# Attention and a gated product on one core: batch 1's score matmuls of two pairs in three visits, one head pair's masks moved to VectorE

## The chip, the cores and the metric

One of the cores of a Trainium2 chip runs the whole program. The time is device time in microseconds (us), the median of three runs. One more execution is profiled, and everything that is said here of single instructions is from that one.

## The reference

Blockwise causal attention over 8 batches, 8 heads, 576 positions and 64 columns a head; its result, laid out as 4608 rows of 512, goes through a gated product with 2048 columns in the middle.

```python
# q, k, v: (8, 8, 576, 64); block = 64
scores = scale * np.matmul(q, k.transpose(0, 1, 3, 2))
mask = (pos[:, None] // block) >= (pos[None, :] // block)
scores = np.where(mask, scores, -1000000000.0)
attn = np.exp(scores - scores.max(-1, keepdims=True))
attn = attn / (attn.sum(-1, keepdims=True) + 1e-09)
x = np.matmul(attn, v).transpose(0, 2, 1, 3).reshape(4608, 512)
# w_in: (512, 2048); w_out: (2048, 512); beta: (2048,)
h = x @ w_in
out = (h * (1.0 / (1.0 + np.exp(-beta * h)))) @ w_out
```

## The kernel before

**The plan.** The program is not written in the order in which it runs. Python code adds operations to a planner `P`: each with its engine, an estimated duration, what it depends on, the tiles that it holds and a priority. The planner picks, engine by engine, the operation that can start and has the lowest priority number, gives tiles their places, and so fixes the order of each engine's instructions. On the chip an engine runs that order from front to back and waits where a semaphore is not yet there: an instruction that waits holds up all behind it.

**Attention.** A pair is two heads, numbered u = 4b + c for batch b and c from 0 to 3, so that batch 0 has pairs 0 to 3 and batch 1 has pairs 4 to 7; the fourth pair is pair 3. The Q and K of batches 0 and 1 come in by one DMA for each of Q and K of a pair, are turned into bfloat16 (L731), transposed by TensorE (L742, four matmuls against an identity) and copied out of PSUM (L752). From batch 2 on (`b >= QB`) they come for two pairs at once and a DMA transposes them (L783, on SyncE's queue).

The scores are computed transposed, keys on the partitions. A pair's scores have four parts by key block: part 0 (512 query columns), part 1 (64 and 448), part 2 (320 and 192) and part 3 (64). The two heads of a pair lie on the two halves of the array's rows, and the code hands the matmuls of both halves out in turn (L837, and L457, which repeats a matmul with weights that are there). What the planner moves as one operation is called a visit here. Where `b` is not in `JOIN`, a pair has two visits, of parts (0, 1) and of parts (2, 3). Where it is, two pairs have three: (0, 1) of the first, (2, 3) of both (the joined visit), (0, 1) of the second. Each visit's parts 0 to 2 need a pair of PSUM banks each, the small part 3 a single one. ScalarE takes the exponential (L857; L872 for part 3), and masks are memsets that put zeros over the blocks above the diagonal (L865, L867): on VectorE, but for the first two parts of batch 0's pairs, which are on GpSimd.

The value product of a pair (L1051, 30 matmuls) holds a pair of banks: banks 0, 2, 4 or 6 on where `b` is in `JOIN`, else 0 or 2 (`pv.at`). VectorE takes the reciprocal of the sums (L1063) and normalises (L1070) into `xq`; TensorE transposes that (L1099, five matmuls) and VectorE copies it into `xT` (L1109). From batch 3 on a DMA transposes `xq` (L1087, SyncE's queue). The last 64 rows of batch 0 are done apart (L975 to L1038, the late rows).

**The gated product** goes in nine chunks of 512 rows. A chunk has sixteen groups of four matmuls of `xT` and a quarter of `w_in` (L1297), each group with one single bank of PSUM (four to seven, in turn as they come free); ScalarE takes a tanh of it (L1307), VectorE combines the two into `gT` (L1311), and then the bank is free. The output of chunk 0 is the product with `w_out` in groups of four matmuls (L1333); other chunks use a scheme of fewer products (L1214, with sums by VectorE, L1178). Groups of chunk 0 fill TensorE between the scores of batch 1; the fifth is the first that needs the second quarter of `w_in`. The quarters of `w_in` (L524) and of `w_out` (L529) are issued on GpSimd's queue, between its casts and masks. A few matmuls on zeros (L548) fill places in which the planner expects TensorE to stand.

Of the kernel before, what the change touches and what calls it, by code (L numbers as in the profile page):

```python
# [11 lines left out]
NPAIR = 4  # L12
# [347 lines left out]
def bass_blockwise_causal_attn__then__act_swish_beta_kernel(  # L360
# [10 lines left out]
    with es:  # L371
# [9 lines left out]
        JOIN = (2,3,4,5,6,7)  # L381
# [271 lines left out]
        copied, more0 = [], []  # L653
        early6, rows = [], []
        QKI, QKX = 550, 2700
        for u in range(NU):
# [10 lines left out]
            if b < QB:  # L667
# [50 lines left out]
                turned = []  # L718
                for w, (nm, src) in enumerate((("Q", q), ("K", k))):
                    ts, pt = P.tile("ST"), P.tile("P1")  # L720
                    early6.append(ts)

                    def fl(g, e, ts=ts, src=src, b=b, c=c):
                        return [g.dma_start(STm[ts.slot].rearrange("p h j d -> p h (j d)"),  # L724
                                            src[b, 2 * c:2 * c + 2, 0:512].rearrange("h (p j) d -> p h (j d)", j=4))]

                    o = ld[nm, u] = P.op("SP", 540, fl, tiles=[ts], xfer=(760, 950)[b], prio=u, dma=["d_S", 0, 1])
                    o.pkt = 48.0

                    def fn(g, e, ts=ts, tn=tn, p=p, w=w):  # L730
                        return g.tensor_copy(QKn[tn.slot][:, p, w, 0:512].rearrange("p (j h d) -> p j h d", j=4, h=2),  # L731
                                             STm[ts.slot].rearrange("p h j d -> p j h d"))

                    onp = u not in (0, 3) or w == 1
                    o = P.op("POOL" if onp else "DVE", 620 if onp else 430, fn, deps=[o], tiles=[ts, tn],
                             prio=-40 + 3 * u if onp else -1)
                    if u == 4:
                        kcast4 = o

                    def ft(g, e, tn=tn, pt=pt, p=p, w=w):  # L740
                        for i in range(4):
                            z = g.transpose(PSb[:, pt.slot, 128 * i:128 * i + 128],  # L742
                                            QKn[tn.slot][:, p, w, 128 * i:128 * i + 128], identB[:])
                        return z

                    o = P.op("PE", 4 * 56, ft, deps=[o, c4], tiles=[tn, pt, tt_], lat=4 * 56 + 170, mode="full",
                             prio=pr(u))

                    def fc(g, e, pt=pt, td=tt_, p=p, w=w):
                        x, y = (QKT[td.slot][:, p, w, 0:512].rearrange("c (p j) -> c p j", j=4),  # L750
                                PSb[:, pt.slot, 0:512].rearrange("c (j p) -> c p j", j=4))
                        return g.activation(x, y, ACT.Copy) if e == "ACT" else g.tensor_copy(x, y)  # L752

                    o.rest = 400.0 if b else 0.0
                    held4 = held4 + [o] if u == 4 else [] if u < 4 else held4
                    held_t = held_t + [o] if u == 5 else [] if u < 5 else held_t

                    turned.append(P.op(("DVE", "ACT") if u in (4, 5) else "DVE", dve_t(512) + 30, fc, deps=[o], tiles=[pt, tt_], prio=-5 if b < 1 else .5))
# [28 lines left out]
            tqk, cps = tt_, turned  # L787
# [3 lines left out]
            if b not in JOIN or p == 0:  # L791
# [6 lines left out]
                for grp in visits:  # L798
# [46 lines left out]
                    o = P.op("PE", n, fq, deps=cps + more, tiles=list({id(x): x for x in pst}.values()) + [tqk] + [tes[uu] for uu in sorted({uu for uu, _ in grp})] * (b > 0),  # L845
# [5 lines left out]
            for g0 in range(4 if b else 3):  # L851
                o, ps = qk[g0]
                if g0 < 3:
# [14 lines left out]
                    zs.append(P.op("DVE" if b or g0 == 2 else "POOL", 160 if g0 != two else 220, fz, deps=[x], tiles=[te], prio=-20 if b or g0 == 2 else -37))  # L868
# [558 lines left out]
```

## Time and profile before

| what | value |
|---|---|
| median of 3 runs | 328.6 us (328.39 to 328.95) |
| the profiled execution: its time | 329.3 us |
| its span | 327.5 us |
| TensorE busy | 316.4 us, 97% |
| VectorE, ScalarE, GpSimd busy | 219.9, 211.8, 84.5 us |
| chain that ended last | 83% TensorE, 5% DMA, 4% VectorE, 4% ScalarE |

The span goes from the first to the last record of the profiled execution; its time is taken around it, on the device too. The chain follows the work that ended last back to what released it, so it tells on which engine the span was spent, and not what a gain there is worth. In rows of the timeline, neighbouring instructions of one line stand together (x4), and a row's length is from the start of the first to the end of the last; since matmuls overlap, a row ends a little after the next has started.

### The profile page before, as it was taken

Reading aid. Unit: us, or ns where it says so; the run is one execution under the profiler, and the core shown is the slowest. Engines: PE = TensorE matmul, PEld = TensorE weight load, DVE = VectorE, ACT = ScalarE, POOL = GpSimd, SP = SyncE. Lnnn points to the kernel's source line nnn. Section 1 sums busy time; section 2 is a strip of 40 time slices with the busy share of each in tenths; the row PEclk is TensorE's granted clock in tenths of the full one; section 3 lists DMA queues with packets and bytes.
Section 4 is the critical chain, followed back from the end, with each engine's and each line's share of the span. In section 5 each row is a group of like instructions: output and inputs, shape, how many; then the busy total and the mean of one; then the engine's idle time right before and its main releaser. Section 6 shows DMA issues by size and latency. Waiting matters only on the chain.

```text
span 327.5 us, 7435 instructions
## 1 busy us (share of the span) xinstructions
PE 316.4 (97%) x3101; PEld 200.3 (61%) x3012; DVE 219.9 (67%) x455; ACT 211.8 (65%) x312; POOL 84.5 (26%) x137
## 2 busy tenths in 40 slices
PE   7698999999999999999999999999999999999996
PEld 2454446445786457854776467666666766666695
DVE  5657857578763789368843996659576866666742
ACT  2769891388557886499657866885978454544521
POOL 4768090073073046103520541150000000000000
PEclk9999999999999999999999999999999999999999
DMA  7999999999999999997999999999030310111023
GB/s 224 225 302 233 215 211 199 169 292 189 226 252 221 222 193 218 186 240 152 196 190 241 231 197 195 199 169 152 0 74 2 104 34 32 62 36 35 6 92 128
DMA packets 156706, 53.58 MB, mean 164 GB/s; under 512 B 139120, under 2 KB 156160, under 8 KB 156672
## 3 DMA queue, kind: packets, MB, share of 16 engines
q1 hardware_dynamic: 144112, 40.46, 65.8%
q10 hardware_dynamic: 8336, 8.46, 8.2%
q0 software_dynamic: 4224, 4.19, 7.8%
q8 instruction: 24, 0.39, 0.5%
q14 instruction: 10, 0.08, 0.1%
HBM read 36.71 MB, written 9.44 MB: 141 GB/s over the span
## 4 chain that ended last, share of the span: by engine, by line
PE 83%; DMA 5%; DVE 4%; ACT 4%; issue 2%; SPq 1%; POOL 1%; POOLq 0%
PE PS L1297 34%; PE PS L1214 29%; PE PS L1051 8%; PE PS L837 6%; PE PS L1333 4%; DMA w_in<-in_moe_w_in_dram 3%; ACT E L857 2%; DMA ST<-in_q_dram 2%; DVE gT L1311 1%; ACT th L1307 1%; DVE QKT L752 1%; SPq L724 1%; DMA xT<-xq 1%; PE PS L1099 1%; PE PS L912 0%
## 5 line engine op out<-in xcount | busy, mean ns | idle before, releaser
L1297 PE MATMUL PS<-xT,w_in 128*128 128x512 bf16 x576 | 137.7, 379 | 3.1 <-DMA w_in<-in_moe_w_in_dram 1.2
L1307 ACT ACTIVATE th<-PS,beta 128x512 f32<-128x512 f32 x144 | 97.0, 701 | 54.9 <-PE PS L1297 53.9
L1311 DVE SCALAR_TENSOR_TENSOR gT<-th,PS 128x512 f16<-128x512 f32 x144 | 95.2, 681 | 35.8 <-ACT th L1307 35.4
L857 ACT ACTIVATE E<-PS 128x1024 bf16<-128x1024 f32 (+1 forms) x90 | 87.5, 1014 | 22.4 <-PE PS L837 21.5
L1297 PEld LDWEIGHTS PS<-xT,w_in 128*128 128x128 bf16 x576 | 53.1, 98 | 58.5 <-issue 2.2
L1214 PE MATMUL PS<-w_out,gT 128*128 128x256 f16 x512 | 63.0, 273 | 0.1
L1214 PEld LDWEIGHTS PS<-w_out,gT 128*128 128x128 f16 x512 | 49.0, 98 | 12.1 <-issue 0.8
L776 POOL CAST QKn<-ST 128x640 bf16<-128x640 f32 x48 | 37.0, 771 | 24.9 <-DMA ST<-in_k_dram 13.9
L624 POOL CAST Vn<-Vs 128x640 bf16<-128x640 f32 x24 | 19.6, 815 | 91.7 <-DMA Vs<-in_v_dram 90.6
L1236 ACT ACTIVATE ost<-PS 128x512 f32<-128x512 f32 x32 | 19.3, 604 | 28.5 <-PE PS L1214 28.5
L1214 PE MATMUL PS<-OV 128*128 128x256 f16 (+1 forms) x264 | 31.8, 270 | 0.0
L1051 PEld LDWEIGHTS PS<-Vn,E 128*128 128x128 bf16 x810 | 27.5, 97 | 3.9 <-issue 0.4
L837 PE MATMUL PS<-QKT 64*128 64x448 bf16 (+7 forms) x292 | 28.6, 295 | 0.5 <-ACT E L857 0.5
L1051 PE MATMUL PS<-Vn,E 128*128 128x65 bf16 x810 | 28.4, 193 | 0.0
L1214 PEld LDWEIGHTS PS<-OV 128*128 128x128 f16 x264 | 24.5, 98 | 6.1 <-issue 0.6
L1178 DVE TENSOR_TENSOR OV<-gT 128x1024 f16<-128x1024 f16 x32 | 23.9, 753 | 0.6
L837 PEld LDWEIGHTS PS<-QKT 64*128 64x128 bf16 (+1 forms) x292 | 13.3, 94 | 17.7 <-issue 3.6
L1070 DVE TENSOR_TENSOR xq<-PS,inv 128x640 bf16<-128x640 f32 x28 | 23.0, 820 | 0.5
L1239 DVE SCALAR_TENSOR_TENSOR ost<-PS,ost 128x512 f32<-128x512 f32 x22 | 15.2, 689 | 9.5 <-PE PS L1214 6.9
L865 DVE MEMSET E<- 64x64 uint32 x57 | 6.3, 112 | 17.9 <-ACT E L857 16.0
L1214 PE MATMUL PS<-OV,gT 128*128 128x256 f16 (+1 forms) x136 | 16.0, 266 | 0.0
L1333 PE MATMUL PS<-w_out,gT 128*128 128x512 f16 x64 | 15.3, 379 | 0.0
(106 smaller groups left out, 189.9 us busy)
## 6 DMA issues: line engine op xcount, KB each, us to landing
out_dram<-ost ACTq DMA_DIRECT2D x32, 256.0 KB, 3.9
ST<-in_q_dram SPq DMA_DIRECT2D x12, 576.0 KB, 6.2
ST<-in_k_dram SPq DMA_DIRECT2D x12, 576.0 KB, 7.2
Vs<-in_v_dram SPq DMA_DIRECT2D x24, 256.0 KB, 4.6
ST<-in_q_dram SPq DMA_DIRECT2D x8, 256.0 KB, 5.9
ST<-in_k_dram SPq DMA_DIRECT2D x8, 256.0 KB, 6.1
w_in<-in_moe_w_in_dram POOLq DMA_DIRECT2D x4, 512.0 KB, 8.4
w_out<-in_moe_w_out_dram POOLq DMA_DIRECT2D x4, 512.0 KB, 8.9
```

The costliest lines, as they stand in the source:

```text
L624: return g.tensor_copy(Vn[t.slot][:, 0:n, g0:g1, 0:64], Vs[ts.slot][:, 0:n, g0:g1, :])
L776: return g.tensor_copy(QKn[tn.slot][:].rearrange("p a w n -> p (a w n)")[:, 640 * (2 * a + w):][:, 0:640] .rearrange("p (t h d) -> p t h d ...
L837: z = g.matmul(o, QKT[tqk.slot][r, uu % 2, 1, k0:k0 + m], x)
L857: return g.activation(E3[es_(te)][:, g0, :, 0:n], PS[:, ps.slot:ps.slot + 2, 0:n], ACT.Exp, scale=0.125)
L1051: z = g.matmul(o, eblk(te, t, i, h), Vn[Tv.slot][:, t, 2 * c + h, 0:65], start=(t == 0), stop=(t == i))
L1070: return g.tensor_tensor(xq[xq_(tx)][:].rearrange("p i (h d) -> p h i d", h=2), both(pv, 0, 64), x, ALU.mult)
L1178: return P.op("DVE", dve_t(SZ * HC / 2), mk(lambda g: g.tensor_tensor(fo(), fx(), fy(), op)), deps=deps, tiles=tiles, prio=prio)
L1214: x = g.matmul(PS[:, pw.slot, HM * w + c0:HM * w + c1], fa()[:, j, 128 * w:128 * w + 128], fb()[:, j, c0:c1], start=first and (pair or w = ...
L1297: z = g.matmul(PS[:, ph.slot, :], w_in[:, c, 128 * j:128 * j + 128], xT[:, c, row % RX:row % RX + RC], start=(c == 0), stop=(c == 3))
L1307: return g.activation(th[tt.slot][:], PS[:, ph.slot, :], ACT.Tanh, scale=beta[:, j:j + 1])
L1311: return g.scalar_tensor_tensor(out=gT[tg.slot][:, j, :], in0=th[tt.slot][:], scalar=1.0, in1=PS[:, ph.slot, :], op0=ALU.add, op1=ALU.mult)
L1333: z = g.matmul(PS[:, po.slot, 0:d1 - d0], gT[tg.slot][:, j, 128 * w:128 * w + 128], w_out[:, j, d0:d1], start=(j == 0), stop=(j == NJ - 1))
```

## The change

Batch 1 is put into `JOIN`. Its scores, until now four pairs of two visits, become twice three. For that the code of batches 0 and 1 makes the loads, casts, transposes and copies of pairs u and u + 1 when it comes to the first of them (`vu`), and the copies are kept by pair (`turns`), so that a visit depends on the copies of its pairs alone. The value products of batch 1 may now take any of four pairs of banks. Apart from it, the masks of pair 3 that GpSimd wrote go to VectorE, with VectorE's priority.

```diff
-        JOIN = (2,3,4,5,6,7)
+        JOIN = (1, 2, 3, 4, 5, 6, 7)
...
-        copied, more0 = [], []
+        copied, more0, turns = [], [], {}
...
-                turned = []
-                for w, (nm, src) in enumerate((("Q", q), ("K", k))):
+                for vu, w, nm, src in [(vu, w, *z) for vu in ((u,) if b not in JOIN else (u, u + 1) if p == 0 else ())
+                                      for w, z in enumerate((("Q", q), ("K", k)))]:
+                    cv, pu_ = vu % NPAIR, vu % 2
...
-                    o = ld[nm, u] = P.op("SP", 540, fl, tiles=[ts], xfer=(760, 950)[b], prio=u, dma=["d_S", 0, 1])
+                    o = ld[nm, vu] = P.op("SP", 540, fl, tiles=[ts], xfer=(760, 950)[b], prio=vu, dma=["d_S", 0, 1])
...
-                    turned.append(P.op(("DVE", "ACT") if u in (4, 5) else "DVE", dve_t(512) + 30, fc, deps=[o], tiles=[pt, tt_], prio=-5 if b < 1 else .5))
+                    turns.setdefault(vu, []).append(P.op(("DVE", "ACT") if vu in (4, 5) else "DVE", dve_t(512) + 30, fc, deps=[o], tiles=[pt, tt_], prio=-5 if b < 1 else .5))
...
-            tqk, cps = tt_, turned
+            tqk = tt_
...
-                    o = P.op("PE", n, fq, deps=cps + more, tiles=list({id(x): x for x in pst}.values()) + [tqk] + [tes[uu] for uu in sorted({uu for uu, _ in grp})] * (b > 0),
+                    o = P.op("PE", n, fq, deps=(turned if b >= QB else [o for uu in sorted({uu for uu, _ in grp}) for o in turns[uu]]) + more, tiles=list({id(x): x for x in pst}.values()) + [tqk] + [tes[uu] for uu in sorted({uu for uu, _ in grp})] * (b > 0),
...
-                    zs.append(P.op("DVE" if b or g0 == 2 else "POOL", 160 if g0 != two else 220, fz, deps=[x], tiles=[te], prio=-20 if b or g0 == 2 else -37))
+                    zs.append(P.op("DVE" if b or g0 == 2 or u == 3 else "POOL", 160 if g0 != two else 220, fz, deps=[x], tiles=[te], prio=-20 if b or g0 == 2 or u == 3 else -37))
```

From the joined loop on, a line of the changed kernel has the number of before plus one (L837 is L838, and so on to the end).

**TensorE, around the second quarter of w_in.** Before, the order has here the fourth L1297 group, pair 4's visit (2, 3), a transpose of pair 5, the fifth group (the first that needs the second quarter), the late rows' value product and the next visit (2, 3), pair 5's.

```order
L1297 MATMUL PS<-xT,w_in 128x512 x4
L837 MATMUL PS<-QKT 128x320 x2
L837 MATMUL PS<-QKT 128x192 x2
L837 MATMUL PS<-QKT 64x64 x2
L742 MATMUL PS<-identB,QKn 128x128 x4
L1297 MATMUL PS<-xT,w_in 128x512 x4
L1007 MATMUL PS<-Vn,gT 128x65 x40
L837 MATMUL PS<-QKT 128x320 x2
L837 MATMUL PS<-QKT 128x192 x2
L837 MATMUL PS<-QKT 64x64 x2
L742 MATMUL PS<-identB,QKn 128x128 x12
```

Now, from the second half of pair 4's visit (0, 1) on, there is the fourth group, a filler, pair 5's last transpose ahead of its scores, the fifth group, the joined visit and two transposes, and then the sixth group.

```order
L1298 MATMUL PS<-xT,w_in 128x512 x4
L548 MATMUL PS<-zero 128x256
L743 MATMUL PS<-identB,QKn 128x128 x4
L1298 MATMUL PS<-xT,w_in 128x512 x4
L838 MATMUL PS<-QKT 128x320 x2
L838 MATMUL PS<-QKT 128x192 x2
L838 MATMUL PS<-QKT 128x320 x2
L838 MATMUL PS<-QKT 128x192 x2
L838 MATMUL PS<-QKT 64x64 x4
L743 MATMUL PS<-identB,QKn 128x128 x8
L1298 MATMUL PS<-xT,w_in 128x512 x4
```

The visit (2, 3) of pair 4 has moved from ahead of the fifth group to behind it, where it is one with pair 5's.

**TensorE, at the end of batch 1.** Before, the last groups of L1297, the four value products and the transposes L1099 alternate, and L1333 starts behind the last value product.

```order
L1297 MATMUL PS<-xT,w_in 128x512 x8
L1051 MATMUL PS<-Vn,E 128x65 x60
L1297 MATMUL PS<-xT,w_in 128x512 x8
L1099 MATMUL PS<-identB,xq 128x128 x5
L1051 MATMUL PS<-Vn,E 128x65 x30
L1099 MATMUL PS<-identB,xq 128x128 x5
L1051 MATMUL PS<-Vn,gT 128x65 x30
L1333 MATMUL PS<-w_out,gT 128x512 x8
L1099 MATMUL PS<-identB,xq 128x128 x5
```

Now three value products stand in a row, the transposes of pairs 4, 5 and 6 follow with one group of L1333 between them, and pair 7's visit (0, 1) comes after those.

```order
L1298 MATMUL PS<-xT,w_in 128x512 x8
L1052 MATMUL PS<-Vn,E 128x65 x90
L1100 MATMUL PS<-identB,xq 128x128 x5
L1334 MATMUL PS<-w_out,gT 128x512 x4
L1100 MATMUL PS<-identB,xq 128x128 x10
L838 MATMUL PS<-OV 128x512 x2
L457 MATMUL PS<-OV 128x64 x2
L838 MATMUL PS<-OV 128x448 x2
L1334 MATMUL PS<-w_out,gT 128x512 x16
```

The two groups of L1297 that stood between the value products now stand ahead of them, and a visit and the fourth value product have moved behind the transposes.

**VectorE, in the same place.** Before, the combines L1311 stand between the reciprocals, normalisations and copies of single pairs.

```order
L1311 SCALAR_TENSOR_TENSOR gT<-th,PS 128x512
L1063 RECIPROCAL inv<-PS 128x10
L1070 TENSOR_TENSOR xq<-PS,inv 128x2x5x64
L1311 SCALAR_TENSOR_TENSOR gT<-th,PS 128x512
L1109 COPY xT<-PS 128x512
L1109 COPY xT<-PS 128x64
L1311 SCALAR_TENSOR_TENSOR gT<-th,PS 128x512
L1063 RECIPROCAL inv<-PS 128x10
L1109 COPY xT<-PS 128x512
L1109 COPY xT<-PS 128x64
L1070 TENSOR_TENSOR xq<-PS,inv 128x2x5x64
```

Now the last combine comes first, and the reciprocals and normalisations of pairs 5 and 6 stand two by two.

```order
L1312 SCALAR_TENSOR_TENSOR gT<-th,PS 128x512
L1064 RECIPROCAL inv<-PS 128x10 x2
L1110 COPY xT<-PS 128x512
L1110 COPY xT<-PS 128x64
L1071 TENSOR_TENSOR xq<-PS,inv 128x2x5x64 x2
L1110 COPY xT<-PS 128x512
L1110 COPY xT<-PS 128x64
L1110 COPY xT<-PS 128x512
L1110 COPY xT<-PS 128x64
```

Both normalisations stand behind the copies of pair 4, and the copies of pairs 5 and 6 behind both.

## Rows read from the trace of the kernel before

**Rows 1.** The page, busy us of each engine (share of the span) and instructions.

```profile
PE 316.4 (97%) x3101; PEld 200.3 (61%) x3012; DVE 219.9 (67%) x455; ACT 211.8 (65%) x312; POOL 84.5 (26%) x137
```

**Rows 2.** TensorE's waits from 45 us on: us in total, times, longest us.

```profile
PE PS L1297 <- DVE xT L1109: 0.6, 1, 0.6
...
PE PS L837 <- ACT E L857: 0.2, 1, 0.2
```

**Rows 3.** Timeline of TensorE near 31 us: start us, us, instruction, [idle <-releaser].

```profile
27.97 1.03 PE L1297 MATMUL PS<-xT,w_in 128*128 128x512 bf16 x4
28.96 0.54 PE L837 MATMUL PS<-QKT 64*128 64x320 bf16 x6
29.43 0.40 PE L742 MATMUL PS<-identB,QKn 128*128 128x128 bf16 x4
31.00 1.04 PE L1297 MATMUL PS<-xT,w_in 128*128 128x512 bf16 x4 [1.18 <-DMA w_in<-in_moe_w_in_dram]
...
34.84 0.39 PE L837 MATMUL PS<-QKT 64*128 64x512 bf16 x2 [0.34 <-ACT E L857]
```

**Rows 4.** Timeline of GpSimd (POOL) ahead of 22 us.

```profile
19.01 0.20 POOL L865 MEMSET gT<- 64x128 bf16 x1
...
19.76 0.62 POOL L731 CAST QKn<-ST 128x512 bf16<-128x512 f32 x1
21.47 0.74 POOL L524 DMA_DIRECT2D w_in<-in_moe_w_in_dram  x1 [1.09 <-DMA ST<-in_k_dram]
```

**Rows 5.** Timeline of TensorE at the end of batch 1.

```profile
43.38 1.04 PE L1297 MATMUL PS<-xT,w_in 128*128 128x512 bf16 x4 [0.40 <-DVE gT L1311]
...
44.89 1.90 PE L1297 MATMUL PS<-xT,w_in 128*128 128x512 bf16 x8
46.62 1.97 PE L1051 MATMUL PS<-Vn,E 128*128 128x65 bf16 x60
...
51.34 0.44 PE L1099 MATMUL PS<-identB,xq 128*128 128x128 bf16 x5
...
52.53 1.89 PE L1333 MATMUL PS<-w_out,gT 128*128 128x512 f16 x8
```

**Rows 6.** Timeline of ScalarE (ACT) in batch 1's scores.

```profile
40.03 1.99 ACT L857 ACTIVATE E<-PS 128x1024 bf16<-128x1024 f32 x2
41.84 1.34 ACT L1307 ACTIVATE th<-PS,beta 128x512 f32<-128x512 f32 x2
...
43.99 1.37 ACT L1307 ACTIVATE th<-PS,beta 128x512 f32<-128x512 f32 x2
```

**Rows 7.** Timeline of TensorE, a joined visit of a later batch.

```profile
117.02 0.67 PE L837 MATMUL PS<-QKT 64*128 64x64 bf16 x12
```

**Rows 8.** Timeline of VectorE (DVE), the combine of the group at 31.00.

```profile
32.80 0.69 DVE L1311 SCALAR_TENSOR_TENSOR gT<-th,PS 128x512 f16<-128x512 f32 x1 [1.24 <-ACT th L1307]
```

**Rows 9.** Timeline of VectorE at the end of batch 1.

```profile
49.74 0.21 DVE L1063 RECIPROCAL inv<-PS 128x10 f32<-128x10 f32 x1
49.99 0.82 DVE L1070 TENSOR_TENSOR xq<-PS,inv 128x640 bf16<-128x640 f32 x1
50.73 0.68 DVE L1311 SCALAR_TENSOR_TENSOR gT<-th,PS 128x512 f16<-128x512 f32 x1
51.33 0.52 DVE L1109 COPY xT<-PS 128x512 bf16<-128x512 bf16 x2
```

**Rows 10.** Timeline of GpSimd, the first issue for w_out.

```profile
40.57 0.74 POOL L529 DMA_DIRECT2D w_out<-in_moe_w_out_dram  x1 [7.74 <-DMA OV<-in_v_dram]
```

**Rows 11.** Timelines of SyncE's queue (SPq) and TensorE, two late waits.

```profile
104.32 1.04 PE L1297 MATMUL PS<-xT,w_in 128*128 128x512 bf16 x4 [0.62 <-DVE xT L1109]
...
162.38 4.81 SPq L783 DMA_TRANSPOSE QKT<-QKn  x1
167.23 2.55 SPq L1087 DMA_TRANSPOSE xT<-xq  x2
...
170.92 1.90 PE L1297 MATMUL PS<-xT,w_in 128*128 128x512 bf16 x8 [0.61 <-DMA xT<-xq]
```

More of the change, by code (lines that the diff above doesn't have):

```diff
@@ L717, in bass_blockwise_causal_attn__then__act_swish_beta_kernel, with fl, fn, ft @@
                     tail = tailc[c // 2]
-                turned = []
-                for w, (nm, src) in enumerate((("Q", q), ("K", k))):
+                for vu, w, nm, src in [(vu, w, *z) for vu in ((u,) if b not in JOIN else (u, u + 1) if p == 0 else ())
+                                      for w, z in enumerate((("Q", q), ("K", k)))]:
+                    cv, pu_ = vu % NPAIR, vu % 2
                     ts, pt = P.tile("ST"), P.tile("P1")
                     early6.append(ts)
-                    def fl(g, e, ts=ts, src=src, b=b, c=c):
+                    def fl(g, e, ts=ts, src=src, b=b, c=cv):
                         return [g.dma_start(STm[ts.slot].rearrange("p h j d -> p h (j d)"),
                                             src[b, 2 * c:2 * c + 2, 0:512].rearrange("h (p j) d -> p h (j d)", j=4))]
-                    o = ld[nm, u] = P.op("SP", 540, fl, tiles=[ts], xfer=(760, 950)[b], prio=u, dma=["d_S", 0, 1])
+                    o = ld[nm, vu] = P.op("SP", 540, fl, tiles=[ts], xfer=(760, 950)[b], prio=vu, dma=["d_S", 0, 1])
                     o.pkt = 48.0
-                    def fn(g, e, ts=ts, tn=tn, p=p, w=w):
+                    def fn(g, e, ts=ts, tn=tn, p=pu_, w=w):
                         return g.tensor_copy(QKn[tn.slot][:, p, w, 0:512].rearrange("p (j h d) -> p j h d", j=4, h=2),
                                              STm[ts.slot].rearrange("p h j d -> p j h d"))
-                    onp = u not in (0, 3) or w == 1
+                    onp = vu not in (0, 3) or w == 1
                     o = P.op("POOL" if onp else "DVE", 620 if onp else 430, fn, deps=[o], tiles=[ts, tn],
-                             prio=-40 + 3 * u if onp else -1)
-                    if u == 4:
+                             prio=-40 + 3 * vu if onp else -1)
+                    if vu == 4:
                         kcast4 = o
-                    def ft(g, e, tn=tn, pt=pt, p=p, w=w):
+                    def ft(g, e, tn=tn, pt=pt, p=pu_, w=w):
                         for i in range(4):
@@ L746, in bass_blockwise_causal_attn__then__act_swish_beta_kernel, with fc @@
                     o = P.op("PE", 4 * 56, ft, deps=[o, c4], tiles=[tn, pt, tt_], lat=4 * 56 + 170, mode="full",
-                             prio=pr(u))
-                    def fc(g, e, pt=pt, td=tt_, p=p, w=w):
+                             prio=pr(vu))
+                    def fc(g, e, pt=pt, td=tt_, p=pu_, w=w):
                         x, y = (QKT[td.slot][:, p, w, 0:512].rearrange("c (p j) -> c p j", j=4),
@@ L754, in bass_blockwise_causal_attn__then__act_swish_beta_kernel @@
                     o.rest = 400.0 if b else 0.0
-                    held4 = held4 + [o] if u == 4 else [] if u < 4 else held4
-                    held_t = held_t + [o] if u == 5 else [] if u < 5 else held_t
-                    turned.append(P.op(("DVE", "ACT") if u in (4, 5) else "DVE", dve_t(512) + 30, fc, deps=[o], tiles=[pt, tt_], prio=-5 if b < 1 else .5))
+                    held4 = held4 + [o] if vu == 4 else [] if vu < 4 else held4
+                    held_t = held_t + [o] if vu == 5 else [] if vu < 5 else held_t
+                    turns.setdefault(vu, []).append(P.op(("DVE", "ACT") if vu in (4, 5) else "DVE", dve_t(512) + 30, fc, deps=[o], tiles=[pt, tt_], prio=-5 if b < 1 else .5))
             elif p == 0:
```

## The prediction

> **What bounds the kernel now.** The page first [rows 1]: TensorE is busy for 316.4 us, 97% of the span of 327.5. Then TensorE's waits from 45 us to the end [rows 2]: four rows, two of 0.6 and two of 0.2 (the first and the last are shown), 1.6 us together. So from there on TensorE hardly stops, and the time is what it has to do, plus what it lost earlier; what it loses earlier is made up only out of those four waits. The loss sits ahead of 45 us, so I read that stretch instruction by instruction.
>
> The first 31 us hang on data. TensorE stands for 1.18 us ahead of 31.00, for the second quarter of w_in [rows 3]. GpSimd issues that load at 21.47, behind a wait of 1.09 us for K's rows [rows 4]. A microsecond of TensorE's work moved from before 31.00 to behind it is therefore lost, since the time it leaves is only waited for longer.
>
> From 31.00 to 52.53, where the first L1333 group starts [rows 3, 5], TensorE does in 21.53 us: twelve groups of L1297, 8 matmuls in 1.73 us (44.89 to 46.62) and so 0.865 a group; seven score visits of batch 1; the four value products (L1051), 0.91 each (51.34 to 52.53 is 1.19, of which the five transposes are 0.28, their row's 0.44 less an overlap of 0.16 into the next row); the late rows of batch 0; the transposes. The rows show two waits in it, 0.34 and 0.40; with the 0.17 by which such a row outlasts the time to the next start (1.90 against 1.73), they cost 0.5 each, 1.0 in all. ScalarE and VectorE are close behind: ScalarE's rows from 40.03 on show no idle time [rows 6].
>
> The profiled execution took 329.3 us, 1.8 more than its span; the median of the three runs is 328.6, 0.7 below it. The sum is made against 329.3, and its difference is then put on 328.6.
>
> **Visits.** A (2,3) visit goes from 28.96 to 29.43, and starts 0.12 after its predecessor is through (27.97 + 0.865 = 28.84): 0.59 us [rows 3]. At 576 columns for each half of the array, 0.24 us, the rest is 0.35. The joined visit of this shape isn't in the trace. It can't be below that of the later batches, whose row lasts 0.67 [rows 7]; less the 0.07 by which the row at 28.96 outlasts its time to 29.43, and with the same lead, that is 0.72. It can't be above two visits (1.18) either. I take one visit and the second pair's 0.24 of columns: 0.83. That saves 0.35 a join, 0.70 for two.
>
> But only three of the four old visits stand behind 31.00: pair 4's was done at 28.96, in time that TensorE had to spare. In the new order no (2,3) visit can come before pair 5's K is turned, and the joined one stands behind the w_in group. Counted from 31.00: before 3 x 0.59 = 1.77, after 2 x 0.83 = 1.66. The gain that counts is 0.11 us (bounds: 0.33 gain, 0.59 loss).
>
> The Trainium skill (TensorEngine Tiling (Array Packing), Key Properties) says that a change of the tiling mode drains TensorE. The 0.35 us that a visit costs beyond its columns agrees. By that rule alone the change is worth 0.70 us; by the rows, 0.11.
>
> **The waits that take its place.** I follow the new order with the durations above.
> - The joined visit ends at 31.87 + 0.83 = 32.70, two transposes of 0.23 follow, and at 33.16 the next L1297 group wants the result bank of the one at 31.00. That bank comes free when VectorE ends its combine, 33.49 [rows 8]: 33.54. Wait 0.38.
> - Two more transposes, the late rows, two groups and pair 5's (0,1) visit bring TensorE to about 37.9. From 38.7 ScalarE has two exponentials, three tanh, two exponentials, three tanh, and for the joined visit two exponentials, each with a small one. By [rows 6] two exponentials take 1.81 (40.03 to 41.84), two tanh and an exponential with its small one 2.15 (41.84 to 43.99), two tanh alone 1.34 less an overlap of 0.18: twice 1.81, twice 2.15 and 1.16 are 9.08 us, to 47.78. The last two tanh come then, ending 48.46 and 49.03. TensorE has the fifteenth group at 45.4, after a wait of 0.1, and the sixteenth ends at 47.2.
> - Now three value products stand in a row (47.2, 48.1, 49.0). The third takes banks 4 and 5, and so waits until VectorE has combined the fifteenth group: its tanh ends 48.46, combine 48.55 to 49.24. Wait 0.3; the third runs 49.28 to 50.19.
> - VectorE then works without a gap, each step by its spacing in [rows 9]: combine 0.60, normalise pair 4 0.74, combine 0.60, two reciprocals 0.25 each, copies 0.52, normalise pair 5 and pair 6 0.74 each. From 48.55 that is pair 5 done at 52.25 and pair 6 at 52.99; with the signal to TensorE I put 52.28 and 53.02. TensorE's own order: pair 4's transposes at 50.19 (0.28), one L1333 group from 50.64 (0.17 after the bank), pair 5's transposes, free at 51.5, wait until 52.28 (0.8), and pair 6's until 53.02 (0.45). Pair 7's (0,1) visit ends at 53.94.
>
> The waits come to 0.38 + 0.1 + 0.3 + 0.17 + 0.8 + 0.45 = 2.2, against 1.0 before. In work, TensorE at 53.94 is where it was before at 52.53 plus one set of transposes and one L1333 group less one value product: 52.53 + 0.28 + 0.865 - 0.91 = 52.77. It is 1.15 us late. Queued behind the waiting transposes are that visit and all L1333 groups; what would have covered them was the interleaving of groups and value products that the order of before has at 46.62 to 52.53. The bounds are 0 (VectorE keeps ahead) and 2.0 (each wait 40% longer).
>
> w_out isn't late: its first quarter is issued at 40.57 [rows 10]. A quarter of w_in, issued at 21.47, was awaited until 31.00 [rows 3, 4], 9.5 us; by that w_out's is there at 50.1, and the new order asks for it near 50.6. If it were later, TensorE would wait for it in place of the 0.17, and the transposes behind it would wait less.
>
> **Masks** (of pair 3, the fourth). GpSimd loses two rows, 19.01 to 19.76 [rows 4], and would reach the w_in issue 0.75 earlier. It still waits there for K's rows, so its 1.09 of idle time hides this; I count 0 (bound 0.75 gain, if the rows of K came earlier too). VectorE gets the masks, at most the 0.75 that they took GpSimd; they stand near 19 us, and what they delay goes into TensorE's 1.18 of waiting for w_in [rows 3], so 0 there too (bound: nothing on the path unless over 1.18).
>
> **Given back later.** Ahead of 104.32 TensorE waited 0.62 for the last copy of batch 2, ahead of 170.92 0.61 for a DMA transpose [rows 11]. At the first the new order puts a joined visit between the transposes and the group, which hides about 0.3. The second is set by SP's queue: the transposes are issued at 167.23, behind another that holds the queue from 162.38 for 4.81 [rows 11]. That queue has its own pace, and a TensorE that comes a microsecond later waits that much less: 0.6 back. I set 0.2 against it for waits that a new order makes elsewhere.
>
> **Sum.** 329.3 + 1.15 - 0.3 - 0.6 + 0.2 = 329.75, a loss of 0.4 to 0.5. On the median: 328.6 + 0.4 = 329.0.
>
> **Rivals.** About 0.2% (0.66 us) is what a measurement of this kernel can tell from no change.
> - *The loss of 1.15 stays whole*: 329.7. The waits at 104 and 170 then come again, because SP's issues follow VectorE, and so TensorE. For it: SP's transposes of xT wait for VectorE's normalise. Against it: the queue before 167.23 is full of its own work.
> - *The drain is what counts*: VectorE keeps ahead at 50 us, so that the six waits are no more than the old 1.0, and the 0.70 of two joins comes through, since the idle time at 31.00 takes other work: 327.9, faster. It decides in favour of this if pair 5's and pair 6's transposes start within 0.3 of the work ahead of them. Against it: VectorE's row of work above has no gap in it.
> - *GpSimd's time was on the path*: w_in lands up to 0.75 earlier, and TensorE's wait of 1.18 shrinks: 327.9 too (with nothing else). Against it stands the 1.09 of idle time. Were the masks and visits to change nothing at all, it would be 328.6.
> - *More is late*: the waits are at their upper bound (2.0), or the late stretch gets new ones: 330.3.
>
> **How the numbers follow.** Chances: forecast 0.40, loss whole 0.25, drain 0.15, GpSimd 0.05, more late 0.15. Of the forecast's 0.40, most lies within 0.66 of no change (0.33), 0.06 above it. The whole loss gives 0.20 slower and 0.05 the same; more late 0.12 and 0.03; the two faster cases 0.16 faster and 0.04 the same. Together 0.17 faster, 0.45 the same, 0.38 slower. The range reaches from the faster rivals to the upper bound of the waits, 327.7 to 330.2, with 0.2 outside; the forecast's own range is 328.5 to 329.6.
>
> **What would show it.** In the changed profile: the w_in group still at 31.0, with the joined visit of some 0.6 to 0.75 right behind it; VectorE without a gap from about 48.5 to 53; waits of the transposes L1100 on VectorE near 51 to 53; the waits at 104 and 170 smaller. I am wrong if the w_in group moves by over 0.3, if those transposes don't wait, or if TensorE's waits after 60 us are over 2 us.

## The result, and the profile after

The changed kernel is slower: 333.54 us, the median of six runs (331.21 to 335.08), against 328.85 in the runs of before beside it. The ratio is 1.0139, with a 95% interval of 1.0096 to 1.0181. I had forecast 329.0 and a range up to 330.2. (Ratios leave disturbed executions out, and so stand a little off the quotient of the medians.)

The profiled execution is the quickest of the six, 331.21. Its span is 329.0 us, so that 2.2 us of its time lie outside the span; before it was 1.8 (329.3 and 327.5). The lines of its page that answer to [rows 1] and to the chain:

```profile
PE 316.9 (96%) x3103; PEld 200.2 (61%) x3013; DVE 221.0 (67%) x456; ACT 211.8 (64%) x313; POOL 85.7 (26%) x135
...
PE 77%; DMA 8%; DVE 7%; ACT 4%; issue 2%; SPq 1%; POOL 0%; ACTq 0%; POOLq 0%
```

TensorE has as much work as before (316.9 against 316.4), and the chain now goes through DMA and VectorE more. Of the 1.5 us by which the span is longer, the next view tells most. TensorE's waits from 45 us to the end, as in [rows 2] (us in total, times, longest):

```profile
PE PS L1298 <- DMA xT<-xq: 2.6, 2, 1.5
PE PS L1100 <- DVE xq L1071: 0.5, 2, 0.3
```

Before, the wait for the DMA transposes of `xT` was one of 0.6. Now there are two, of 2.6 together.

The early stretch, TensorE's timeline from the w_in group (the first that needs the second quarter of w_in, at 29.89) to the first large L1334 row (52.48), which answers to [rows 3, 5]:

```profile
29.89 1.04 PE L1298 MATMUL PS<-xT,w_in 128*128 128x512 bf16 x4 [0.35 <-DMA w_in<-in_moe_w_in_dram]
30.86 0.79 PE L838 MATMUL PS<-QKT 64*128 64x320 bf16 x12
31.59 0.62 PE L743 MATMUL PS<-identB,QKn 128*128 128x128 bf16 x8
32.44 1.04 PE L1298 MATMUL PS<-xT,w_in 128*128 128x512 bf16 x4 [0.23 <-DVE gT L1312]
...
49.53 1.02 PE L1334 MATMUL PS<-w_out,gT 128*128 128x512 f16 x4
50.82 0.45 PE L1100 MATMUL PS<-identB,xq 128*128 128x128 bf16 x5 [0.27 <-DVE xq L1071]
51.55 0.45 PE L1100 MATMUL PS<-identB,xq 128*128 128x128 bf16 x5 [0.28 <-DVE xq L1071]
...
52.48 3.63 PE L1334 MATMUL PS<-w_out,gT 128*128 128x512 f16 x16
```

The joined visit starts 0.105 after its predecessor is through (29.89 + 0.865) and ends at 31.59: 0.835 us. The transposes of pairs 5 and 6 wait at 50.82 and 51.55 for VectorE. VectorE's timeline in that place, as in [rows 9], shows what it does meanwhile:

```profile
49.31 0.29 DVE L1064 RECIPROCAL inv<-PS 128x10 f32<-128x10 f32 x2
49.51 0.52 DVE L1110 COPY xT<-PS 128x512 bf16<-128x512 bf16 x2
49.95 1.54 DVE L1071 TENSOR_TENSOR xq<-PS,inv 128x640 bf16<-128x640 f32 x2
51.41 1.15 DVE L1110 COPY xT<-PS 128x512 bf16<-128x512 bf16 x4
```

No row has idle time. From 29.89 to 52.48 TensorE takes 22.59 us. For the same work the order of before takes 31.00 to 52.53, and 0.235 more for one set of transposes and one group less one value product: 21.77. So the end of batch 1 loses 0.82 us here.

The late stretch, TensorE's timeline at the first groups of two chunks and at the two value products between them:

```profile
171.19 1.90 PE L1298 MATMUL PS<-xT,w_in 128*128 128x512 bf16 x8 [1.46 <-DMA xT<-xq]
...
187.09 1.97 PE L1052 MATMUL PS<-Vn,E 128*128 128x65 bf16 x60
...
202.91 1.04 PE L1298 MATMUL PS<-xT,w_in 128*128 128x512 bf16 x4 [1.15 <-DMA xT<-xq]
```

The row at 171.19 answers to 170.92 in [rows 11]; the wait has grown from 0.61 to 1.46. TensorE comes to it 0.58 earlier than before (169.73 against 170.31), and goes on 0.27 later. The wait at 202.91 is new. Why, SyncE's queue tells. Before:

```profile
186.54 3.13 SPq L1087 DMA_TRANSPOSE xT<-xq  x1
189.72 0.58 SPq L765 DMA_DIRECT2D ST<-in_k_dram  x1
190.60 5.57 SPq L783 DMA_TRANSPOSE QKT<-QKn  x1
196.21 1.28 SPq L1087 DMA_TRANSPOSE xT<-xq  x1
```

After, in the same place:

```profile
186.56 2.81 SPq L766 DMA_DIRECT2D ST<-in_k_dram  x1
189.42 4.00 SPq L598 DMA_DIRECT2D Vs<-in_v_dram  x1
193.47 4.01 SPq L784 DMA_TRANSPOSE QKT<-QKn  x1
197.52 2.60 SPq L1088 DMA_TRANSPOSE xT<-xq  x2
```

Before, one transpose of `xT` is issued at 186.54 and the next at 196.21. Now both stand at 197.52, behind a load of V with a row of 4.00 us and a transpose of Q and K with one of 4.01. For these two the queue waits for GpSimd's casts (L777), as its own waits from 185 to 206 us show (us in total, times, longest):

```profile
SPq L784 <- POOL QKn L777: 3.4, 1, 3.4
SPq L598 <- POOL QKn L777: 1.9, 1, 1.9
```

Before, the transpose of Q and K waits 3.7 for such a cast there, with one transpose of `xT` already ahead of it.

### The profile page after: what moved, and what is told of

Same layout as the page of the kernel before. It is cut to its first block, busy times and chain, and to the rows that moved or that the text cites. A ratio compares the mean times of both kernels' runs of the same rounds, so it can differ in the third digit from the quotient of the medians.

```text
span 329.0 us, 7427 instructions
## 1 busy us (share of the span) xinstructions
PE 316.9 (96%) x3103; PEld 200.2 (61%) x3013; DVE 221.0 (67%) x456; ACT 211.8 (64%) x313; POOL 85.7 (26%) x135
## 4 chain that ended last, share of the span: by engine, by line
PE 77%; DMA 8%; DVE 7%; ACT 4%; issue 2%; SPq 1%; POOL 0%; ACTq 0%; POOLq 0%
PE PS L1298 34%; PE PS L1215 27%; PE PS L1052 6%; PE PS L838 5%; PE PS L1334 4%; DMA ST<-in_q_dram 4%; DMA w_in<-in_moe_w_in_dram 3%; ACT E L858 2%; DVE gT L1312 2%; DMA xT<-xq 2%; ACT th L1308 2%; DVE xq L1071 1%; DVE QKT L753 1%; SPq L725 1%; DVE gT L1179 1%
## 5 line engine op out<-in xcount | busy, mean ns | idle before, releaser
L1298 PE MATMUL PS<-xT,w_in 128*128 128x512 bf16 x576 | 137.1, 379 | 3.9 <-DMA xT<-xq 2.6
L1298 PEld LDWEIGHTS PS<-xT,w_in 128*128 128x128 bf16 x576 | 53.0, 98 | 59.5 <-DMA xT<-xq 3.2
L777 POOL CAST QKn<-ST 128x640 bf16<-128x640 f32 x48 | 38.3, 799 | 21.6 <-DMA ST<-in_k_dram 12.4
L838 PE MATMUL PS<-QKT 64*128 64x448 bf16 (+8 forms) x292 | 28.4, 295 | 0.2 <-ACT E L858 0.2
L1179 DVE TENSOR_TENSOR OV<-gT 128x1024 f16<-128x1024 f16 x32 | 24.8, 784 | 0.6
L838 PEld LDWEIGHTS PS<-QKT 64*128 64x128 bf16 (+1 forms) x292 | 13.3, 94 | 17.9 <-issue 3.6
L1334 PE MATMUL PS<-w_out,gT 128*128 128x512 f16 x64 | 14.5, 379 | 0.1
```

The lines of the kernel that those rows point to most:

```text
L777: return g.tensor_copy(QKn[tn.slot][:].rearrange("p a w n -> p (a w n)")[:, 640 * (2 * a + w):][:, 0:640] .rearrange("p (t h d) -> p t h d ...
L838: z = g.matmul(o, QKT[tqk.slot][r, uu % 2, 1, k0:k0 + m], x)
L1179: return P.op("DVE", dve_t(SZ * HC / 2), mk(lambda g: g.tensor_tensor(fo(), fx(), fy(), op)), deps=deps, tiles=tiles, prio=prio)
L1298: z = g.matmul(PS[:, ph.slot, :], w_in[:, c, 128 * j:128 * j + 128], xT[:, c, row % RX:row % RX + RC], start=(c == 0), stop=(c == 3))
L1334: z = g.matmul(PS[:, po.slot, 0:d1 - d0], gT[tg.slot][:, j, 128 * w:128 * w + 128], w_out[:, j, d0:d1], start=(j == 0), stop=(j == NJ - 1))
```

## The experiments

Each kernel was run in five rounds beside the kernel before. In the list, "order from 165 us" means that the planner was given, for each engine, the row of operations that another kernel's plan has from there on; where a table of such rows was put in, line numbers are shifted (L1342, L1343 or L1365 are then the changed kernel's L1298). Some matmuls are missing from the records of these profiles (3068 on TensorE in the changed kernel again, 3103 before). Where a row has x3, x7 or x11, it is as a rule the first, and the wait shown ahead of the row then holds that matmul's 0.2 us too.

| kernel | median us | ratio to before, 95% interval |
|---|---|---|
| the changed kernel again | 333.96 | 1.0144 (1.0104 to 1.0185) |
| joins without the move of the masks | 332.05 | 1.0107 (1.0076 to 1.0138) |
| masks alone | 329.34 | 1.0024 (0.9997 to 1.0052) |
| changed, order of before from 165 us | 331.54 | 1.0095 (1.0068 to 1.0123) |
| changed, order of before from 136 us | 330.77 | 1.0055 (1.0028 to 1.0082) |
| before, changed order from 165 us | 331.17 | 1.0048 (1.0013 to 1.0083) |
| changed, xT first in the queue | 332.46 | 1.0102 (1.0053 to 1.0151) |
| changed, load of V behind xT | 331.33 | 1.0077 (1.0042 to 1.0112) |
| changed, groups ahead of waiting transposes | 333.81 | 1.0135 (1.0095 to 1.0175) |
| the same with order of before from 136 us | 330.33 | 1.0033 (1.0013 to 1.0054) |
| join of pairs 6 and 7 alone | 330.03 | 1.0014 (0.9984 to 1.0045) |
| join of pairs 4 and 5 alone | 329.85 | 1.0017 (0.9993 to 1.0042) |
| before, xT behind the transpose of Q and K | 329.26 | 1.0004 (0.9976 to 1.0032) |
| before, xT behind V and that transpose | 330.22 | 1.0016 (0.9991 to 1.0042) |

**The changed kernel again**, without an edit. 

> The changed kernel once more, for a second profile and the granted clock of each run. Theory A (the loss sits late: the plan after 160 us puts value products and DMA transposes of xT later, and TensorE waits for them near 171 and 203): 331 to 335 us, the profile again has waits for xT near 171 and 203 of about 1 us or more each, and where a run's mean clock is under 1, the stretch at 1.2 GHz stands behind such a wait. Theory B (the loss sits at the end of batch 1, as I had predicted): the same time, but the low clock or the longer waits stand between 45 and 60 us.

Its profiled execution is a long one (335.02, span 332.7). TensorE's timeline at the marks:

```profile
31.14 1.04 PE L1298 MATMUL PS<-xT,w_in 128*128 128x512 bf16 x4 [1.23 <-DMA w_in<-in_moe_w_in_dram]
...
53.73 3.63 PE L1334 MATMUL PS<-w_out,gT 128*128 128x512 f16 x16
...
172.80 1.67 PE L1298 MATMUL PS<-xT,w_in 128*128 128x512 bf16 x7 [2.00 <-DMA xT<-xq]
...
205.36 1.48 PE L1298 MATMUL PS<-xT,w_in 128*128 128x512 bf16 x3 [2.21 <-DMA xT<-xq]
```

Set beside the first profile (span 329.0), the 3.7 us more are: the w_in group 1.25 later; the stretch from there to 53.73 the same 22.59; the wait for `xT` at 172.80 0.54 longer, that at 205.36 1.06 longer; and behind 205.36 to the end 127.34 us against 126.09, 1.25 more. The rest of the stretches together are 0.4 shorter. (Both rows lack a matmul, so that the two waits are rather 0.3 and 0.8 longer.) What the 1.25 is, the busy time by windows shows (length, busy us of PE, PEld, DVE, ACT, POOL with the number of instructions, then the granted clock, the DMA share and GB/s):

```profile
205.30:208.70 3.40, 3.34 (x12) 0.95 (x10) 0.69 (x1) 1.53 (x2) 0.00 (x0) 0.50 1.03 194
208.70:212.00 3.30, 3.30 (x27) 1.91 (x24) 1.20 (x4) 2.67 (x5) 0.00 (x0) 1.00 1.14 232
```

Behind the wait of 2.21 the granted clock is 0.50 (1.2 GHz) for 3.4 us, and the three matmuls of L1298 there take 1.48, where three take 0.81 in other profiles (at 203.52 below). Theory A's places hold. The six runs of the first measurement have mean clocks of 0.984 to 1.0; so have runs of before, so that the mean clock doesn't tell the two kernels apart.

**Joins alone, masks alone.** One has the whole change but its last hunk (only the line of `JOIN` is shown), the other that last hunk alone:

```diff
-        JOIN = (2,3,4,5,6,7)
+        JOIN = (1, 2, 3, 4, 5, 6, 7)
...
-    zs.append(P.op("DVE" if b or g0 == 2 else "POOL", ...
+    zs.append(P.op("DVE" if b or g0 == 2 or u == 3 else "POOL", ...
```

> The change without the move of pair 3's masks, which stay on GpSimd; the planner's order behind 60 us is the same as in the changed kernel. Theory A: as slow as the changed kernel, 331 to 335, ratio 1.00 to it within 0.3%. If the masks on VectorE cost something, it is nearer to the kernel before, 329 to 331. If they bring w_in earlier, it is slower than the changed kernel by up to 1 us.

> The kernel before with only the move of the masks; the order behind 70 us is that of before. Theory A and my prediction: 328.2 to 329.0, no change that can be measured. If the masks on VectorE are the cost, 330 or more.

The joins alone are slower by 1.07%, and their profile has the wait near 203 too (1.87). The interval overlaps with that of the whole change, and the masks alone make no difference that the ratio shows. But one cost of theirs shows in the spans on record: in every execution of the kernels with the masks of pair 3 on VectorE, the time is 2.18 to 2.32 us above the span, and in every one of the kernels with them on GpSimd, that of before among them, 1.75 to 1.88. So the move costs 0.4 us outside the span, where no row tells why. What else the masks add stays open.

**The late order taken from the other kernel.** The table holds the operations of each engine; the planner may start one only when its predecessor in the table has started:

```diff
+        for e, row in LATE_ORDER.items():
+            for i, k in enumerate(row):
+                made[-k].engs = (e,)
+                made[-k].turn = made[-row[i - 1]] if i else None
         P.schedule()
...
+                        if o.turn is not None and o.turn.start is None:
+                            continue
```

> The changed kernel up to about 165 us of the plan, and behind that each engine's order as in the kernel before (the planner may start a late operation only behind its predecessor of that order; nothing is left out). Theory A: the wait near 203 is gone (0.3 us at most), the span is 327.3 to 328.2 and the time 328.3 to 329.5. Theory B, or a cost that lies in the clock whatever the late order: 331 or more.

> The changed kernel up to about 136 us of the plan, behind that each engine's order as before (nothing is left out). Theory A: like the kernel whose order is that of before from 165 us on (331.5), or better by up to 1 us, since the wait near 171 is that of before too (0.6); 330.3 to 331.5, with no wait for xT over 1 us. Theory C: 331.5 or more, with the waits for xT still there.

> The kernel before up to about 165 us of the plan, and behind that each engine's order as the changed kernel has it (nothing is left out). Theory A (the late order, in which two DMA transposes of xT stand on SyncE's queue behind a transpose of Q and K that waits for GpSimd's casts, costs the time, whatever comes ahead): slower than before by 1 to 3 us, 329.8 to 332, with a wait of TensorE for xT of 1 to 2.5 us near 200 to 205. Theory C (the late order costs nothing by itself; it is the lateness of batch 1 that makes the queue late): within 0.5 us of before.

In the changed kernel the late order of before is worth 2.4 us from 165 us on and 3.2 from 136 us on by the medians (333.96 less 331.54 and 330.77). The intervals of the ratios overlap a little for the first and are apart for the second. In both profiles no wait for `xT` of over 0.2 us is left at either place. The first was expected at 328.3 to 329.5 and came at 331.54: so the late order is not the whole loss. The reverse, the changed order behind the early part of before, costs 0.48%. But six of its twelve executions took 328.99 to 330.06, no more than executions of before, and the others 332.28 to 336.38. The profiled one is of the others (333.8), and shows the wait in another place than I expected:

```profile
174.07 2.63 PE L1342 MATMUL PS<-xT,w_in 128*128 128x512 bf16 x7 [4.41 <-DMA xT<-xq]
```

TensorE stands for 4.41 us at the chunk near 171, and not near 203, where it then comes late enough. That is not the late order's doing: up to 186 us SyncE's queue has its rows in the order of before here, and only issues the transposes of `xT` later (170.16 against 167.23). So this profile doesn't show what the late order costs without the early part of the change.

**Two edits of SyncE's queue in the changed kernel.** Only these rows of the order differ:

```diff
 load of K            (ST)
+2 transposes of xT               (first edit: to here)
 load of V            (Vs)
 transpose of Q and K (QKT)
-2 transposes of xT
+load of V                        (second edit: from above to here)
 transpose of Q and K (QKT)
```

> The changed kernel with one edit of the order of SyncE's queue: the two DMA transposes of xT near 198 us stand ahead of the load of V and of the transpose of Q and K, not behind. Everything else is in the order of the changed kernel (nothing is left out). Theory A, with the queue's order as the mechanism: TensorE's wait near 203 is under 0.3 us, and the time is 1 to 2.5 us under that of the changed kernel, 331.2 to 332.8. If it is TensorE's or VectorE's late order that makes the wait, it stays over 1 us and the time stays near 333.7.

> The changed kernel with one move in SyncE's queue: the load of V that stands near 189 us ahead of the transpose of Q and K goes behind the two DMA transposes of xT; these stay behind the transpose of Q and K. Everything else is in the order of the changed kernel (nothing is left out). If the load of V is what makes them late (it holds the queue for about 4 us there): the wait near 203 is under 0.7 us and the time 331 to 332.8, like the kernel with the transposes of xT first. If the transpose of Q and K alone does it, the wait stays over 1 us and the time near 333.7.

TensorE's timeline of the first edit:

```profile
172.60 1.67 PE L1343 MATMUL PS<-xT,w_in 128*128 128x512 bf16 x7 [1.14 <-DMA xT<-xq]
...
201.56 1.91 PE L1260 MATMUL PS<-OV 128*128 128x256 f16 x16
203.52 0.81 PE L1343 MATMUL PS<-xT,w_in 128*128 128x512 bf16 x3
```

The group that waited 1.15 and 2.21 us follows the L1260 row of 201.56 without a wait. The wait at 172.60 is still there. The median is 1.1 to 1.5 under that of the changed kernel, but the intervals overlap widely, so that a gain in time is not shown. The second edit gives SyncE's queue:

```profile
187.54 2.86 SPq L812 DMA_DIRECT2D ST<-in_k_dram  x1
192.18 5.18 SPq L830 DMA_TRANSPOSE QKT<-QKn  x1
197.41 2.60 SPq L1134 DMA_TRANSPOSE xT<-xq  x2
```

The wait near 203 is gone too, and the median is 331.33, 2.2 to 2.6 under the changed kernel (the intervals just overlap). But the transposes of `xT` are issued no earlier than in the first profile of the changed kernel (197.41 against 197.52): without V ahead, the transpose of Q and K waits the longer for GpSimd's cast, 4.3 us. What differs is that they land 2.6 and 2.8 us after their issue, not 2.9 and 4.0, and that TensorE, which has waited 2.04 near 171 in this profile, comes to the group 0.9 later (about 202.6 against 201.76). So V's place changed here how soon they landed, not when they were issued, and how much of the wait V makes by itself stays open.

**The same queue order in the kernel before**, first without and then with V ahead:

```diff
-transpose of xT
 load of K
+load of V                        (second kernel only)
 transpose of Q and K
+transpose of xT
 transpose of xT
```

> The kernel before with one edit of the order of SyncE's queue, the reverse of the one that took the wait near 203 away: the two DMA transposes of xT that are issued near 187 and 196 us stand behind the transpose of Q and K that is issued near 191, as in the changed kernel. All other engines have the order of before (nothing is left out). Theory A with the queue's order as the mechanism: TensorE waits 1 to 2.5 us for xT near 200, and the time is 1 to 2.5 us over that of before. If the queue's order alone does not decide, within 0.5 us of before.

> The kernel before with SyncE's order near 190 us as in the changed kernel: load of V, transpose of Q and K, then the two DMA transposes of xT; all other engines in the order of before (nothing is left out). If the queue's order with V is the mechanism: TensorE waits 1 to 2.5 us for xT near 201, and the time is 1 to 2.5 us over that of before, 330 to 331.5. If the wait comes only together with TensorE's new late order, it is under 0.7 us and the time within 0.5 us of before.

Neither costs anything that shows. The second one's queue:

```profile
187.94 3.34 SPq L644 DMA_DIRECT2D Vs<-in_v_dram  x1
191.32 4.25 SPq L829 DMA_TRANSPOSE QKT<-QKn  x1
195.62 2.65 SPq L1133 DMA_TRANSPOSE xT<-xq  x2
```

The order of these rows is that of the changed kernel, but V is issued at 187.94 and not at 189.42 (191.66 in the second profile of the changed kernel), and the transposes of `xT` at 195.62 and not at 197.52 (199.94). So the order of these rows alone doesn't make the wait. That it does together with the lateness that the rest of the new order brings to the queue is what is left, and was not tried by itself.

**The end of batch 1.** Two groups of L1334 go ahead of the transposes that wait, two more ahead of pair 7's value product:

```diff
 transposes of pair 4
 group of L1334
+group of L1334
 transposes of pair 5
+group of L1334
 transposes of pair 6
 visit (0, 1) of pair 7
-2 groups of L1334
...
```

> The changed kernel with one edit of TensorE's order at the end of batch 1: two groups of L1334 are moved ahead of the transposes of pairs 5 and 6, where TensorE waited for VectorE's normalising (0.27 and 0.28 us), and two more ahead of pair 7's value product. Everything else is in the order of the changed kernel (nothing is left out). My prediction's step (those waits cost) gives: the two waits are under 0.1, the groups behind start 0.5 earlier than in the changed kernel counted from the w_in group. If the late queue takes it all back, the time stays within 0.5 us of the changed kernel (333 to 334); if what is saved early comes through, it is 0.5 less.

> The changed kernel with both mends: two groups of L1334 ahead of the waiting transposes at the end of batch 1, and from about 136 us of the plan on the order of before (nothing is left out). If what is saved early comes through when the late queue does not hold TensorE: 0.4 to 0.6 us under the kernel with the second mend alone (330.8), about 330.3. If it is taken back again, 330.8 or more.

TensorE's timeline of the first kernel, at the end of batch 1 and at the two late waits:

```profile
51.53 1.89 PE L1401 MATMUL PS<-w_out,gT 128*128 128x512 f16 x8
53.55 0.45 PE L1167 MATMUL PS<-identB,xq 128*128 128x128 bf16 x5
53.84 1.03 PE L1401 MATMUL PS<-w_out,gT 128*128 128x512 f16 x4
54.71 0.44 PE L1167 MATMUL PS<-identB,xq 128*128 128x128 bf16 x5
...
173.65 1.67 PE L1365 MATMUL PS<-xT,w_in 128*128 128x512 bf16 x7 [2.61 <-DMA xT<-xq]
...
205.98 0.81 PE L1365 MATMUL PS<-xT,w_in 128*128 128x512 bf16 x3 [1.98 <-DMA xT<-xq]
```

No transpose waits for `xq`, and counted from the w_in group the groups behind come about 0.5 earlier, as expected. But the time is that of the changed kernel (333.81): the waits for `xT` are 2.61 and 1.98. With the order of before behind 136 us, where those waits are 0.34 and none, the kernel is at 330.33, against 330.77 without the early mend. The intervals overlap, so that 0.44 is of the size expected, but not shown.

**One join at a time.** The condition `b not in JOIN` is narrowed for batch 1 to the pairs 6 and 7 (`c >= 2`), or to 4 and 5 (`c < 2`). From about 70 us on the planner then gives each engine the order of the kernel before by itself, without any table.

```diff
-            if b not in JOIN or p == 0:
+            if not (b in JOIN and (b > 1 or c >= 2)) or p == 0:
```

> The change with only one of the two joins: pairs 6 and 7 of batch 1 in three visits, pairs 4 and 5 in two each as before, value products of batch 1 on the banks of before. The masks are on VectorE. From about 70 us on each engine has the order of the kernel before (nothing is left out). Theory A (what costs is mainly the late order that the planner makes out of the change): within 0.5 us of before, since the late order is that of before; or faster by up to 0.4, the worth of one join by the rows. Theory B (the joined visits cost at the end of batch 1, and that comes through): slower by 0.5 to 1.5 us.

> The other join alone: pairs 4 and 5 in three visits, pairs 6 and 7 in two each, masks on VectorE, order of the kernel before from about 70 us on (nothing is left out). Theory A: within 0.5 us of before, no gain, since only one of the two old visits (2, 3) that it replaces stood behind the w_in group. Theory B: slower by 0.5 to 1.5 us.

Neither is told from the kernel before. TensorE's timeline with pairs 4 and 5 joined shows that early waits are there, and that the late one shrinks:

```profile
31.29 1.04 PE L1298 MATMUL PS<-xT,w_in 128*128 128x512 bf16 x4 [1.24 <-DMA w_in<-in_moe_w_in_dram]
...
34.06 0.81 PE L1298 MATMUL PS<-xT,w_in 128*128 128x512 bf16 x3 [0.45 <-DVE gT L1312]
...
49.10 2.89 PE L1052 MATMUL PS<-Vn,E 128*128 128x65 bf16 x90 [0.58 <-DVE gT L1312]
...
171.42 1.67 PE L1298 MATMUL PS<-xT,w_in 128*128 128x512 bf16 x7 [0.43 <-DMA xT<-xq]
```

0.45 and 0.58 us are waited in batch 1, but 0.43 only at the chunk near 171, where it was 0.61. That is the way in which I had expected the whole change to give a loss back. It is no proof, since in other profiles with the late order of before this wait reads from none to 0.96.

## Why the prediction was wrong

**What bounds the kernel.** Right in the first 60 us and too simple behind them. I read the time as TensorE's work plus its loss ahead of 45 us. The queue of SyncE, of which I had said that it has its own pace, is a second bound up to the last such wait, near 205 us: where it comes late, TensorE loses anew.

**Visits: right.** The joined visit was put at 0.83 and took 0.835.

**Masks, w_in: right within what an execution varies, but for a term that I put at nothing.** I had the w_in group at 31.0; it is at 29.89, 30.05 and 31.14 in three profiles of kernels with the joins. The first figure is over the 0.3 that I had named as a sign of error, the last is not, so the quarter's landing varies by about a microsecond and no gain of the masks is shown. The sum took the 1.8 us between time and span over from before without a reason; with the masks on VectorE they are 2.2 in every execution.

**The waits that take its place: right in mechanism, 0.33 too large.** Sum 1.15, measured 0.82 (0.80 to 0.92 in six more profiles with this order). VectorE works without a gap from 47.2 to 52.5, the places are those named, and one term was far off: pair 5's transposes wait 0.43 with the signal, not 0.8.

**Given back later: this is the step that failed.** At 104 the wait is 0.34, as said. At 171 I took off 0.6, since SyncE's queue would keep its pace. That holds where the order from 136 us on is that of before: the transposes are issued at 167.29 (before 167.23), TensorE comes 1.7 later, and no wait is left of the 0.6. With the planner's new order the wait grew by 0.85 and 1.39 in two profiles. In the first, 0.58 of the growth is that TensorE came earlier than before; in the second TensorE came 0.5 later and the queue later still. And for "waits that a new order makes elsewhere" I had 0.2: they are 1.15 at 202.91, and in the longer execution 2.21 with 1.25 of lower clock behind it; all four profiles of kernels with both joins, the new late order and no edit of the queue have this wait (1.15 to 2.21), and none with the late order of before has it. My own sign of error, over 2 us of waits after 60 us, came. I had not looked at the order behind 60 us. There two value products stand together at 187.09, where before one started at 180.13 and one at 188.59, and the transposes of `xT` that follow from them have gone behind V and the transpose of Q and K, which waits for GpSimd.

The sum on the longer profile, against the span of before (332.7 less 327.5, 5.2): w_in 0.14 later, end of batch 1 0.82, from there to the wait at 171 TensorE 0.47 quicker, that wait 1.39 more, wait near 205 2.21, clock 1.25, the remainder 0.14 less: 5.2. The rival "more is late" had the direction, with new waits in the late stretch, but at 330.3.

**What is shown and what is open.** Shown is that each join alone leaves the time as it was, within some 0.45%, where the late order stays, that the late order is worth 0.9% from 136 us on in the changed kernel (0.5% from 165 us on, with intervals that overlap), that the wait near 203 comes with the new late order and is gone in the profile of either edit of the queue, and that the move of the masks costs 0.4 us (0.13%) outside the span. Open is how the rest of the remaining 0.3 to 0.55% divides. A wait for VectorE's normalising near 96 us, 0.4 to 1.0 in six of the nine profiles with both joins, 0.16 in one and none in two, and the end of batch 1 are candidates of the right size. No kernel has both joins and the order of before from 70 us on, as the single joins have it, so that the early part of both is not tested by itself. Open too is the size of the wait at 171, which differs between executions of one order (1.46 and 2.00, and 0.21 with the joins alone), whether the masks add more, and which part of the wait near 203 is V, which the casts on GpSimd and which the lateness ahead of both.

The Trainium skill (TensorE: Matmul & The Clock Gate, What's actually happening) says that TensorE's clock is at 1.2 GHz when it has been idle and at 2.4 when busy. The 0.50 behind the wait of 2.21 agrees. In the kernel with the groups moved ahead the waits of 2.61 and 1.98 were followed by no such fall, so a wait of that size may or may not cost it.

## What to carry to other kernels

A list scheduler turns an edit at 30 us into a new order at 200 us: compare the whole orders, those of DMA queues above all, before any saving is counted, and look for transfers that have moved behind others on a queue that runs in order. A loss is made up in a later wait only if what is waited for keeps its time; where the queue itself waits for engines that are late, the wait can move along or grow. Look at the time outside the span too: here a move of a few memsets cost 0.4 us there. To judge an edit, hold the order elsewhere fixed and run it so as well: here either join by itself makes no difference that shows, and both cost 1.4% with what the planner made of them.

## What the runs showed of the hardware

Two additions of VectorE (L1179 into OV) take 2.32 us where a cast of V on GpSimd is under way when they start, in the kernel with the joins alone; VectorE's row, and GpSimd's:

```profile
89.34 2.32 DVE L1179 TENSOR_TENSOR OV<-gT 128x1024 f16<-128x1024 f16 x2
```

```profile
88.92 4.11 POOL L624 CAST Vn<-Vs 128x640 bf16<-128x640 f32 x4 [10.45 <-DMA Vs<-in_v_dram]
```

In the second profile of the changed kernel the cast starts when the second addition is under way:

```profile
90.44 1.28 DVE L1179 TENSOR_TENSOR OV<-gT 128x1024 f16<-128x1024 f16 x2
```

```profile
91.17 4.20 POOL L624 CAST Vn<-Vs 128x640 bf16<-128x640 f32 x4 [10.41 <-DMA Vs<-in_v_dram]
```

The nine profiles with both joins agree. Where the cast starts ahead of both additions, they take 2.32 or 2.33 (three profiles); where it starts between them, 1.80 or 1.81 (two); where it starts behind the start of the second, 1.28 or 1.29 (four). So an addition that starts beside the running cast takes about 0.5 us longer here, and one that had already started takes no longer. TensorE's wait near 96 us follows: 0.98 in the first three, 0.61 and 0.62 in the next two, and 0.43, 0.16 and twice none in the others. No edit moved the cast, so that it causes the wait is likely, but not tried.
